# An S5 scan with a sparse feed-forward: one weight block by a turning transfer, selected tokens turned by a transfer

## The chip, the cores and the metric

The kernel runs on one core of a Trainium2 chip. The core has five engines with queues of their own: PE (TensorE, matrix products; the profile gives its weight loads apart as PEld), DVE (VectorE), ACT (ScalarE), POOL (GpSimd) and SP (SyncE), which here only issues transfers. Transfers ("DMA") run on 16 DMA engines. The metric is device time in microseconds (us). Three runs of the kernel before took 252.46, 252.49 and 252.91 us; the median is 252.49 us.

## The reference

Input `A_x` has 2048 tokens of width 1024. All arrays are bfloat16.

```
xn  = layernorm(x)
# A: diagonal complex state space, P = 1024 states
Bu  = xn @ B_bar.T                       # complex, 2048 x 1024
h_t = Lam_bar * h_(t-1) + Bu_t           # scan over the tokens
yA  = 2 * Re(h @ C.T) + xn * Dskip
# B: feed-forward for the 2 tokens with the greatest xn @ w_r
idx = argsort(-(xn @ w_r))[:2]
y   = (silu(xn[idx] @ w_gate) * (xn[idx] @ w_up)) @ w_down * sigmoid(r[idx])
yB  = xn;  yB[idx] += y
out = x + yA + yB
```

## The kernel before, in words

The 2048 tokens are cut into 16 chunks `c` of 128 tokens, and two chunks make one of 8 frames `f`. The names below are the task names of the table `ORDER`; a task is one small function that emits a few instructions, and the program is emitted in the order of that table. Each engine works its own instructions off in that order, so one late input holds up all that stands behind it on the engine.

For each chunk `x.c` loads the tokens, `bs.c`, `bn.c` and `rstd.c` (chunks 0 to 5; for the others `sum.c` and `sq.c` on ACT) find mean and variance, and `apply.c` writes the normalized tokens `xn`. They are turned, so that features lie on partitions: chunks 0 to 3 by products with the identity on PE (`Tpe.c`, emptied by `xnT.c` on ACT), the others by a turning transfer from SP (`T.c`).

The weights `B` are needed turned as well: `BT[ri][j]`, with `ri` 0 for the real and 1 for the imaginary part, and `j` for one of 8 blocks of 128 states. Tasks `B.j.ri` with `j` from 1 load them with a turning transfer (`load_B`, L235, the operation DMA_TRANSPOSE). Block 0 comes by two plain transfers into `Bn` (L176); `tB.ri` turns each part with 8 products on PE (L257) and `B.0.ri` copies it out of PSUM on ACT (L260). The weights `C` are loaded by four larger turning transfers (`C.dh.ri`, L240).

`Bu.f.j` (L668) is the product for one frame and one block of states: 16 matmuls. `u.f.j` copies it out of PSUM, `TI.f` rotates it (L723, L725), `SC.c.ri` is the scan along the tokens (L751; L744 in the last chunk), `gb.c.ri` narrows it, `TO.c` rotates back (L793, L795) and `Y.c.q` (L880) is the product with `C`: four quarters of 8 matmuls a chunk. The carry from chunk to chunk goes through POOL (`cw`, `cy`, `cin`). The output is seeded in PSUM by ACT (`seed`), and `xm.c` (L870) and `ADD.c.dh` (L891) on DVE, and `out.c.dh` (L895) finish it.

For part B, `r.0` and `r.1` are the router's products, and `cand` and `idx` on DVE find the two tokens (L941 to L979). `gather` fetches their rows, `bns` (L284, L286), `rstds` and `norm` (L1014) normalize them, `sT` turns them with 8 small products on PE (L1020) into PSUM, and `xT` on DVE clears the tile `xselT` and copies the turned rows in (L1026, L1027). `mm.i` are the products with the three large weights (L1068 gate and up, L1099 down); their tiles `w.n` are loaded from SP (L1056) into four slots that earlier tiles must have left. The result must reach the output rows of two tokens that are known only at run time. For all chunks but the last ones `fix` on POOL adds it in memory, by an indirect transfer (L1118) that waits for the stores of these chunks. For the last ones (`c >= UPD_C`) a one-hot matrix `hot` (L983 to L987) adds it in PSUM, by a product `hotY.c.dh` (L885); their stores wait for `fix`. `UPD_C` is 14, so chunks 14 and 15 go this way.

Of the kernel before, what the change touches and what calls it, by code (L numbers as in the profile page):

```python
# [29 lines left out]
xnT.3 bs.5 Bh.1.0.0 B.5.0 first Bh.1.0.1 u.0.2 Bu.1.0 cos B.4.1 Bu.1.1 bn.5 bs.4 sin bn.4 B.5.1 u.1.0 Bu.1.2 log B.6.0 den nmean.5 nmean.4 sq1.0 kappa  # L30
x.6 Bu.0.3 sq1.1 inv.0 u.1.1 rc.0 rstd.5 Bu.0.4 R0.0 rstd.4 apply.5 u.1.2 nmr.4 apply.4 T.5 inv.1 nmr.5 tan.0 Bu.1.3 nmr1.4 R.0 nmr.0 u.0.3 B.6.1 rc.1
u.0.4 ntan.0 Bu.1.4 tan.1 u.1.3 T.4 cs ntan.1 Bu.1.5 TI.0.0 xnT.5 Drow u.1.4 sum.7 B.7.0 Bu.1.6 nmean.7 u.1.5 B.7.1 ts.1.0 sq.7 cin.0.0 xnT.4 ends
ts.0.0 Bu.0.5 xr.0 ts.1.1 u.1.6 xr.1 sum.6 E2c.0 C.1.0 Bu.0.6 ts.0.1 nmean.6 sq.6 R0.1 R.1 rstd.6 Bu.0.7 SC.0.0.0 u.0.5 u.0.6 SC.0.0.1 cw.0.0 Bu.1.7
u.0.7 xs.0 E2s.1 C.0.0 cy.0.0 Bu.2.0 TI.0.4 seed.0.0 cin.1.0 u.1.7 seed.0.1 Bu.2.1 E2n.0 E2c.1 nmr.6 cin.0.4 u.2.0 nmr1.5 Bu.2.2 E2s.0 gb.0.0.1 C.0.1
u.2.1 SC.0.4.0 E2n.1 Bu.2.3 gb.0.0.0 SC.0.4.1 u.2.2 cw.0.4 rstd.7 gb.0.4.0 SC.1.0.0 Bu.2.4 cy.0.4 gb.0.4.1 SC.1.0.1 gb.1.0.0 cin.1.4 nmr.7 Bu.2.5
u.2.3 TO.0.0 u.2.4 apply.6 cw.1.0 Bu.2.6 apply.7 cy.1.0 TO.0.4 T.6 seed.1.0 Bu.2.7 x.8 u.2.5 SC.1.4.0 T.7 nmr1.7 Y.0.0 SC.1.4.1 gb.1.4.0 C.1.1 E2t.1
xm.0 E2t.0 cin.2.0 Y.0.1 TI.1.0 gb.1.0.1 xnT.6 xs.1 cw.1.4 Y.0.2 gb.1.4.1 cy.1.4 u.2.6 xnT.7 sum.8 Bu.3.0 x.9 cin.2.4 nmean.8 x.12 u.2.7 xr.3 sq.8
ADD.0.0 x.10 r.0 TO.1.0 out.0.0 rstd.8 Bu.3.1 seed.1.1 SC.2.0.0 u.3.0 xr.2 Bu.3.2 u.3.1 sum.9 SC.2.0.1 cw.2.0 Y.0.3 nmr1.8 gb.2.0.0 Bu.3.3 TO.1.4
gb.2.0.1 cy.2.0 nmr.8 apply.8 Bu.3.4 cin.3.0 xm.1 u.3.2 ADD.0.1 nmean.9 TO.2.0 sq.9 out.0.1 Y.1.0 T.8 rstd.9 u.3.3 x.11 Y.1.1 seed.2.0 xs.2 SC.3.0.0
Y.1.2 xnT.8 sum.12 Y.1.3 ADD.1.0 cw.3.0 u.3.4 SC.3.0.1 gb.3.0.0 out.1.0 Y.2.0 nmr.9 seed.2.1 xm.2 gb.3.0.1 cy.3.0 Y.2.1 ADD.1.1 nmean.12 TI.2.0  # L40
apply.9 out.1.1 cin.4.0 Bu.3.5 seed.3.0 T.9 sq.12 Bu.3.6 rstd.12 nmr.12 apply.12 Bu.3.7 SC.4.0.0 u.3.5 T.12 xnT.9 u.3.6 xs.3 Y.2.2 w.0 SC.4.0.1 cw.4.0
x.15 u.3.7 gb.4.0.0 Y.2.3 TO.3.0 gb.4.0.1 cy.4.0 xnT.12 Bu.4.0 sum.10 cin.5.0 nmean.10 sq.10 Bu.4.1 ADD.2.0 ADD.2.1 seed.3.1 Bu.4.2 SC.5.0.0 out.2.1
rstd.10 out.2.0 nmr.10 nmr1.6 xr.4 u.4.0 Y.3.0 w.1 u.4.1 xr.5 u.4.2 xm.3 cw.5.0 sum.11 SC.5.0.1 Y.3.1 nmean.11 sq.11 Y.3.2 ADD.3.0 cy.5.0 apply.10
TO.4.0 out.3.0 gb.5.0.0 Bu.4.3 T.10 cin.6.0 gb.5.0.1 Y.3.3 u.4.3 rstd.11 TI.3.0 seed.4.0 Bu.4.4 xnT.10 seed.4.1 nmr1.9 sum.15 Bu.4.5 nmr.11 nmean.15
xs.4 Bu.4.6 ADD.3.1 SC.6.0.0 out.3.1 seed.5.0 xr.6 u.4.4 Y.4.0 u.4.5 apply.11 SC.6.0.1 cw.6.0 Y.4.1 gb.6.0.0 T.11 sq.15 x.13 TO.5.0 Y.4.2 cy.6.0 x.14
gb.6.0.1 rstd.15 cin.7.0 Y.4.3 nmr.15 apply.15 xnT.11 xm.4 Bu.4.7 ADD.4.0 ADD.4.1 seed.5.1 SC.7.0.0 Y.5.0 xs.5 u.4.6 xr.7 Bu.5.0 sum.13 T.15 SC.7.0.1
cw.7.0 w.2 Y.5.1 u.5.0 w.3 u.4.7 w.4 xm.5 cy.7.0 seed.6.0 out.4.1 TO.6.0 Y.5.2 w.5 nmean.13 sq.13 cin.8.0 xnT.15 gb.7.0.1 Y.5.3 rstd.13 nmr.13 ADD.5.0
nmr1.13 Bu.5.1 gb.7.0.0 TI.4.0 sum.14 Bu.5.2 u.5.1 nmean.14 apply.13 Y.6.0 sq.14 T.13 SC.8.0.0 Bu.5.3 rstd.14 u.5.2 nmr1.11 nmr.14 Y.6.1 SC.8.0.1
cw.8.0 u.5.3 apply.14 xnT.13 Bu.5.4 gb.8.0.0 T.14 ADD.5.1 cy.8.0 TO.7.0 out.5.1 Bu.5.5 u.5.4 out.4.0 cin.9.0 out.5.0 Bu.5.6 u.5.5 gb.8.0.1 xnT.14
Bu.5.7 TO.8.0 u.5.6 Bu.6.0 u.5.7 xs.6 r.1 nmr1.10 xm.6 u.6.0 seed.6.1 ADD.6.0 Bu.6.1 cand xs.7 xr.8 w.6 seed.7.0 w.7 Y.6.2 out.6.0 u.6.1 nmr1.12  # L50
seed.7.1 Y.6.3 idx Y.7.0 xm.7 gather sig ADD.6.1 sig1 out.6.1 seed.8.0 Bu.6.2 SC.9.0.0 xr.9 Y.7.1 SC.9.0.1 gb.9.0.0 Y.7.2 xs.8 cw.9.0 ADD.7.0 gb.9.0.1
Bu.6.3 TI.5.0 cy.9.0 out.7.0 seed.8.1 u.6.2 Y.7.3 cin.10.0 u.6.3 Bu.6.4 bns Y.8.0 u.6.4 ADD.7.1 rstds xm.8 out.7.1 Bu.6.5 norm xr.10 SC.10.0.0 Y.8.1
xs.9 cw.10.0 sT nmr1.14 Bu.6.6 u.6.5 xT SC.10.0.1 seed.9.0 mm.0 TO.9.0 gb.10.0.1 cy.10.0 Y.8.2 w.8 gb.10.0.0 w.9 ymb0 w.10 u.6.6 w.11 Y.8.3 cin.11.0
w.12 xm.9 ADD.8.0 Bu.6.7 ADD.8.1 seed.9.1 SC.11.0.0 out.8.1 seed.10.0 Y.9.0 w.13 out.8.0 SC.11.0.1 Y.9.1 gb.11.0.0 cw.11.0 mm.1 ADD.9.0 gb.11.0.1
cy.11.0 TO.10.0 Y.9.2 seed.10.1 w.14 cin.12.0 exp.0 w.15 w.16 w.17 Bu.7.0 u.6.7 w.18 xs.10 w.19 gu.0 xr.11 Bu.7.1 u.7.0 out.9.0 gT.0 hot TI.6.0 Bu.7.2
u.7.1 Y.9.3 u.7.2 mm.2 ADD.9.1 SC.12.0.0 Bu.7.3 w.20 exp.1 out.9.1 xr.12 seed.11.0 w.21 Y.10.0 SC.12.0.1 cw.12.0 w.22 w.23 w.24 Y.10.1 w.25 xm.10
gb.12.0.1 cy.12.0 TO.11.0 Y.10.2 u.7.3 gb.12.0.0 cin.13.0 xs.11 Y.10.3 ADD.10.0 Bu.7.4 ADD.10.1 gu.1 xm.11 mm.3 u.7.4 SC.13.0.0 Bu.7.5 w.26 w.27
out.10.0 SC.13.0.1 gb.13.0.0 cw.13.0 out.10.1 Bu.7.6 w.28 seed.11.1 w.29 seed.12.0 w.30 gT.1 Bu.7.7 cy.13.0 xr.13 exp.2 TO.12.0 w.31 u.7.5 cin.14.0
Y.11.0 gb.13.0.1 u.7.6 xs.12 Y.11.1 gu.2 gT.2 mm.4 ADD.11.0 TO.13.0 seed.12.1 Y.11.2 w.32 exp.3 w.33 out.11.0 u.7.7 xr.14 Y.11.3 nmr1.15 w.34 w.35
Y.12.0 ADD.11.1 xm.12 out.11.1 seed.13.0 TI.7.0 Y.12.1 mm.5 Y.13.0 w.36 w.37 ADD.12.0 w.38 SC.14.0.0 w.39 Y.12.2 w.40 w.41 out.12.0 Y.12.3 SC.14.0.1  # L60
gb.14.0.0 cw.14.0 seed.13.1 Y.13.1 gu.3 gb.14.0.1 cy.14.0 gT.3 ADD.12.1 Y.13.2 xs.13 TO.14.0 cin.15.0 seed.14.0 Y.13.3 mm.6 xm.13 ADD.13.0 mm.7
# [1119 lines left out]
```

## Time and profile before

| | |
|---|---|
| median of three runs | 252.49 us |
| the profiled execution, whole | 252.6 us |
| its span, first to last instruction | 250.8 us |
| PE busy | 244.7 us, 98% |
| DVE busy | 238.7 us, 95% |
| ACT busy | 176.0 us, 70% |
| POOL busy | 103.1 us, 41% |
| granted TensorE clock | 1.000 of full speed (the level of 2.4 GHz) |

Times in the rows are counted from the span's start. The profiled execution lies 1.8 us above its span, and 0.1 us above the median of the runs. A share of busy time is a mean over the whole program; where an engine waits and for whom is read from the views below.

### The profile page before, as it was taken

Reading aid. Unit: us, or ns where it says so; the run is one execution under the profiler, and the core shown is the slowest. Engines: PE = TensorE matmul, PEld = TensorE weight load, DVE = VectorE, ACT = ScalarE, POOL = GpSimd, SP = SyncE. Lnnn points to the kernel's source line nnn. Section 1 sums busy time; section 2 is a strip of 40 time slices with the busy share of each in tenths; the row PEclk is TensorE's granted clock in tenths of the full one; section 3 lists DMA queues with packets and bytes.
Section 4 is the critical chain, followed back from the end, with each engine's and each line's share of the span. In section 5 each row is a group of like instructions: output and inputs, shape, how many; then the busy total and the mean of one; then the engine's idle time right before and its main releaser. Section 6 shows DMA issues by size and latency. Waiting matters only on the chain.

```text
span 250.8 us, 5086 instructions
## 1 busy us (share of the span) xinstructions
PE 244.7 (98%) x1995; PEld 165.3 (66%) x1995; DVE 238.7 (95%) x284; ACT 176.0 (70%) x303; POOL 103.1 (41%) x132
## 2 busy tenths in 40 slices
...
GB/s 206 248 227 178 189 212 247 222 186 288 52 105 46 103 123 214 44 108 83 246 235 85 22 230 67 21 63 240 344 358 319 343 241 390 338 351 288 107 44 42
DMA packets 66532, 46.75 MB, mean 186 GB/s; under 512 B 45890, under 2 KB 52424, under 8 KB 66508
## 3 DMA queue, kind: packets, MB, share of 16 engines
...
q0 software_dynamic: 96, 0.01, 0.0%
...
## 4 chain that ended last, share of the span: by engine, by line
PE 84%; ACT 5%; DVE 5%; DMA 3%; SPq 1%; issue 0%
PE pY L880 44%; PE pB L668 35%; PE pG L1068 3%; DMA BT<-in_A_B_im_dram 2%; DVE st L310 1%; PE pD L1099 1%; ACT u L674 1%; DMA xt<-in_A_x_dram 1%; PE r_ps L409 1%; ACT xnT L395 1%; DVE ot L891 1%; DVE xn L339 1%; DVE E1t L551 1%; ACT L522 1%; ACT L519 1%; SPq L235 0%
## 5 line engine op out<-in xcount | busy, mean ns | idle before, releaser
L668 PE MATMUL pB<-xnT,BT 128*128 128x256 bf16 (+1 forms) x1072 | 116.3, 268 | 0.4 <-DMA BT<-in_A_B_im_dram 0.4
L880 PE MATMUL pY<-CT,hT 128*128 128x512 bf16 (+1 forms) x528 | 115.0, 373 | 0.0
L668 PEld LDWEIGHTS <-BT 128*128 128x128 bf16 x1072 | 100.4, 98 | 16.7 <-issue 1.3
L880 PEld LDWEIGHTS <-hT 128*128 128x128 bf16 x528 | 51.2, 98 | 55.0 <-issue 1.5
L767 POOL TENSOR_TENSOR cw<-gf,tL 128x16 f32<-128x16 f32 (+1 forms) x34 | 37.2, 1098 | 92.2 <-DVE gf L751 91.4
L751 DVE TENSOR_TENSOR_SCAN gf<-R,v 128x1040 f32<-128x1040 f32 (+1 forms) x34 | 68.6, 2055 | 0.3
L757 ACT CAST gb<-gf 128x1024 bf16<-128x1024 f32 (+1 forms) x34 | 31.7, 941 | 21.5 <-DVE gf L751 21.2
L674 ACT CAST u<-pB 128x512 bf16<-128x512 f32 x64 | 36.0, 579 | 12.8 <-PE pB L668 12.7
L856 ACT ACTIVATE pY<-xr,nmr_all,rstd_all 128x512 f32<-128x512 bf16 (+1 forms) x33 | 25.0, 763 | 14.7 <-DVE ot L891 11.4
L793 DVE TENSOR_TENSOR m<-gb,E 128x4096 bf16<-128x4096 bf16 x13 | 29.6, 2279 | 0.1
L891 DVE TENSOR_TENSOR ot<-pY,ot 128x512 bf16<-128x512 f32 (+1 forms) x33 | 21.4, 663 | 2.2 <-PE pY L880 1.3
L865 ACT ACTIVATE ot<-xr,nmr_all,rstd_all 128x1024 bf16<-128x1024 bf16 x16 | 19.8, 1238 | 1.9 <-DMA out_dram<-ot 1.8
L782 POOL CAST v<-cy 128x16 bf16<-128x16 f32 (+1 forms) x17 | 18.6, 1096 | 5.0 <-DVE gf L751 4.1
L795 DVE TENSOR_TENSOR hT<-m 128x2048 bf16<-128x2048 bf16 x13 | 15.9, 1225 | 0.4
L725 DVE TENSOR_TENSOR v<-u,m 128x4096 bf16<-128x4096 bf16 x7 | 16.0, 2292 | 0.2
L723 DVE TENSOR_TENSOR m<-u,E1t 128x4096 bf16<-128x4096 bf16 x7 | 16.0, 2283 | 0.0
L783 POOL TENSOR_TENSOR v<-cy,v 128x16 bf16<-128x16 f32 (+1 forms) x17 | 14.5, 851 | 1.4
L775 POOL TENSOR_TENSOR cy<-cw 128x16 f32<-128x16 f32 (+1 forms) x17 | 13.9, 816 | 1.3
L350 ACT ACTIVATE xn<-xt,nmr_all,rstd_all 128x1024 bf16<-128x1024 bf16 x10 | 12.3, 1237 | 0.1
L325 ACT ACTIVATE xn<-xt,nmean_all 128x1024 bf16<-128x1024 bf16 x10 | 11.5, 1146 | 0.2
L870 DVE TENSOR_TENSOR ot<-ot,Drow 128x1024 bf16<-128x1024 bf16 x16 | 10.9, 682 | 0.0
L319 ACT ACTIVATE xn<-xt 128x1024 bf16<-128x1024 bf16 x10 | 10.6, 1056 | 0.0
...
## 6 DMA issues: line engine op xcount, KB each, us to landing
...
out_dram<-ot SPq DMA_DIRECT2D x31, 128.0 KB, 1.7
...
xt<-in_A_x_dram SPq DMA_DIRECT2D x2, 128.0 KB, 2.3
...
```

The costliest lines, as they stand in the source:

```text
L668: nc.tensor.matmul(out=pB[:, ri, ts_], lhsT=BT[ri][j][:, k, :], rhs=xnT_frame(f)[:, k, ts_], start=(k == 0), stop=(k == DT - 1))
L674: nc.scalar.copy(out=u_tiles[f][:, :, :, j, :].rearrange("p c i t -> p i c t"), in_=pB_tiles.pop((f, j))[:].rearrange("p i (c t) -> p i c ...
L723: nc.vector.tensor_tensor(out=m[:].rearrange("p c i j t -> p c (i j t)"), in0=u[:].rearrange("p c i j t -> p c (i j t)"), in1=E1t[:].rearr ...
L751: nc.vector.tensor_tensor_scan(out=flat(gf), data0=flat(R[:, js, :]), data1=flat(v[:, ri, js, :]), initial=0.0, op0=ALU.mult, op1=ALU.add)
L757: nc.scalar.copy(out=gb_tiles[c][:, ri, js, :], in_=gf_tiles[c, js.start, ri][:, :, 2:])
L767: nc.gpsimd.tensor_tensor(out=cw_tiles[c, js.start][:, ri, :, 0:n], in0=g.unsqueeze(1).to_broadcast([128, 2, n]), in1=tL[:, ri, :, js], op ...
L782: nc.gpsimd.tensor_copy(out=v[:, :, js, 0], in_=cy[:, :, 0:n])
L793: nc.vector.tensor_tensor(out=m[:].rearrange("p k i j t -> p k (i j t)"), in1=E2[:].rearrange("p k i j t -> p k (i j t)"), in0=flat(gb[:]) ...
L856: nc.scalar.activation(out=pY[:, 0:d_.stop - d_.start], in_=y_tiles["xr", c][:, d_], func=ACT.Identity, bias=nmr_all[:, c:c + 1], scale=rs ...
L865: nc.scalar.activation(out=y_tiles["ot", c][:], in_=y_tiles["xr", c][:], func=ACT.Identity, bias=nmr_all[:, c:c + 1], scale=rstd_all[:, c: ...
L880: nc.tensor.matmul(out=pY, lhsT=h_tiles[c][:, ri, j, :], rhs=CT[ri][h][:, j, d0:d0 + w], start=False, stop=end, skip_group_check=True)
L891: nc.vector.tensor_add(out=ot, in0=y_tiles.pop(("pY", c, dh))[:, 0:d_.stop - d_.start], in1=ot)
```

## The change

Five things are changed together.

1. Only the real part of the first block of `B` comes by a plain transfer. The imaginary part `BT[1][0]` is loaded by a turning transfer from SP, as the other blocks are; `tB.1` and its copy on ACT go.
2. The selected tokens are turned by a transfer from SP (`sT`, out of 32 rows that `xz` on POOL clears beforehand); the 8 products on PE and the clearing and copying on DVE go.
3. `UPD_C` is 15: chunk 14 has no product with the one-hot matrix, `fix` waits for chunk 14's stores also, and only chunk 15's stores wait for `fix`.
4. The turned tile of chunk 1 lies in the PSUM slot `T`, no longer in one of the three slots of `Bu`. The statistics of chunks 2 to 5 stand behind `apply.1`.
5. The whole table `ORDER` is another one.

```diff
-xa x.0 Bn.0 Bn.1 start.0 warm.0 warm.1 warm.2 warm.3 warm.4 warm.5 warm.6 warm.7 bs.0 pre x.2 warm.8 B.1.0 x.1 bn.0 warm.9 warm.10 bs.1 rstd.0 nmean.0
+warm.0 warm.1 warm.2 warm.3 warm.4 warm.5 warm.6 warm.7 x.0 warm.8 warm.9 warm.10 warm.11 start.0 warm.12 xa bs.0 bn.0 x.1 warm.13 bs.1 rstd.0 applyA
...
-    Bn = work.tile([128, 2, D], BF16, name="Bn", tag=f"F{NSF}")
-    for ri in range(2):
-        nc.sync.dma_start(out=Bn[:, ri, :], in_=(A_B_re, A_B_im)[ri][0:128, :])
+    Bn = work.tile([128, D], BF16, name="Bn", tag=f"F{NSF}")
+    nc.sync.dma_start(out=Bn[:], in_=A_B_re[0:128, :])
...
-    for ri in range(2):
-        add(("Bn", ri), "none", 5.45 + 0.65 * ri, lambda: None, key=-1, takes=[(f"F{NSF}", "Bn", [("tB", 0), ("tB", 1)])])
...
+    add(("Bn", 0), "none", 5.45, lambda: None, key=-1, takes=[(f"F{NSF}", "Bn", [("tB", 0)])])
+    add(("tB", 0), "PE", 0.45, turn_B, [("Bn", 0), ("warm", NWARM - 1), ("pP", 0)], key=-60, takes=[("pB", ("tB", 0), [("B", 0, 0)])])
+    add(("B", 0, 0), "ACT", 1.0, evac_B, [("tB", 0)], key=-60)
+    add(("B", 0, 1), "SP", 1.35, lambda: load_B(1, 0), [("pre",)], key=-89.92, mb=0.31, lag=1.2)
...
-        pT_tiles[c] = psum.tile([128, DT, 128], BF16, name="pT", tag="B" if c == 1 else "misc" if odd else "T", bufs=3 if c == 1 else 1)
+        pT_tiles[c] = psum.tile([128, DT, 128], BF16, name="pT", tag="misc" if odd and c > 1 else "T")
...
-    UPD_C = NCH - CPF
+    UPD_C = NCH - 1
...
+    def sel_zero():
+        ms["xnsel"] = xnp.tile([128, D], BF16, name="xnsel", tag="xn")
+        nc.gpsimd.memset(ms["xnsel"][0:32, :], 0.0)
+
     def sel_T():
-        ms["pX"] = psum.tile([128, DT, 2], BF16, name="pX", tag="misc")
-        for j in range(DT):
-            nc.tensor.transpose(out=ms["pX"][:, j, :], in_=ms["xnsel"][:, j * 128:(j + 1) * 128], identity=ident[0:2, 0:2])
-
-    def sel_xT():
         mw = xin.tile([128, D], BF16, name="mw", tag="xt")
...
-        nc.vector.memset(ms["xselT"], 0.0)
-        nc.vector.tensor_copy(out=ms["xselT"][:, :, 0:2], in_=ms["pX"][:])
+        nc.sync.dma_start_transpose(out=ms["xselT"], in_=ms["xnsel"][0:32, :].rearrange("t (do di) -> t do di", di=128))
```

**What the new order moves on SP at the start.** Transfers as SP issues them, from the second token chunk on; `BT_j` is block `j` (the number behind it is the tile's), `xt` a chunk of tokens. Before:

```order
L165 DMA xt<-in_A_x_dram 128x1024
L176 DMA Bn<-in_A_B_re_dram 128x1024
L176 DMA Bn<-in_A_B_im_dram 128x1024
L231 DMA xt<-in_A_x_dram 128x1024
L235 DMA_TRANSPOSE BT_1_116<-in_A_B_re_dram 128x8x128
L231 DMA xt<-in_A_x_dram 128x1024
L235 DMA_TRANSPOSE BT_1_124<-in_A_B_im_dram 128x8x128
L235 DMA_TRANSPOSE BT_2_117<-in_A_B_re_dram 128x8x128
L235 DMA_TRANSPOSE BT_2_125<-in_A_B_im_dram 128x8x128
L231 DMA xt<-in_A_x_dram 128x1024
```

And now, from the same transfer on:

```order
L164 DMA xt<-in_A_x_dram 128x1024
L174 DMA Bn<-in_A_B_re_dram 128x1024
L229 DMA xt<-in_A_x_dram 128x1024
L233 DMA_TRANSPOSE BT_0_122<-in_A_B_im_dram 128x8x128
L233 DMA_TRANSPOSE BT_1_115<-in_A_B_re_dram 128x8x128
L229 DMA xt<-in_A_x_dram 128x1024
L233 DMA_TRANSPOSE BT_1_123<-in_A_B_im_dram 128x8x128
L233 DMA_TRANSPOSE BT_2_116<-in_A_B_re_dram 128x8x128
L233 DMA_TRANSPOSE BT_2_124<-in_A_B_im_dram 128x8x128
L233 DMA_TRANSPOSE BT_5_119<-in_A_B_re_dram 128x8x128
L229 DMA xt<-in_A_x_dram 128x1024
```

One plain transfer has gone, and one turning transfer has come in ahead of the other blocks; the next chunk of tokens (`x.5` before, `x.4` now) stands one block later.

**On SP up to the last block of B.** From `B.5.1` to `B.7.1`; `xnT<-xn` are `T.5` and `T.4`, `Drow` is the row `Dskip`. Before:

```order
L235 DMA_TRANSPOSE BT_5_128<-in_A_B_im_dram 128x8x128
L235 DMA_TRANSPOSE BT_6_121<-in_A_B_re_dram 128x8x128
L231 DMA xt<-in_A_x_dram 128x1024
L401 DMA_TRANSPOSE xnT<-xn 128x8x128
L235 DMA_TRANSPOSE BT_6_129<-in_A_B_im_dram 128x8x128
L401 DMA_TRANSPOSE xnT<-xn 128x8x128
L861 DMA Drow<-in_A_Dskip_dram 128x1024
L235 DMA_TRANSPOSE BT_7_122<-in_A_B_re_dram 128x8x128
L235 DMA_TRANSPOSE BT_7_130<-in_A_B_im_dram 128x8x128
```

And now:

```order
L233 DMA_TRANSPOSE BT_5_127<-in_A_B_im_dram 128x8x128
L399 DMA_TRANSPOSE xnT<-xn 128x8x128
L233 DMA_TRANSPOSE BT_6_120<-in_A_B_re_dram 128x8x128
L233 DMA_TRANSPOSE BT_6_128<-in_A_B_im_dram 128x8x128
L399 DMA_TRANSPOSE xnT<-xn 128x8x128
L233 DMA_TRANSPOSE BT_7_121<-in_A_B_re_dram 128x8x128
L233 DMA_TRANSPOSE BT_7_129<-in_A_B_im_dram 128x8x128
```

`Drow` stands behind the last block now, and chunk 6's tokens (`x.6`) ahead of this piece.

**On DVE around TO.8 and the choice of tokens.** L793 with L795 is a `TO` (L791 with L793 in the changed kernel), L941 begins `cand`, the scans are called gf<-R,v. Before, from `TO.7`:

```order
L793 TENSOR_TENSOR m<-gb,E_136 128x4096
L795 TENSOR_TENSOR hT<-m 128x2048
L793 TENSOR_TENSOR m<-gb,E_136 128x4096
L795 TENSOR_TENSOR hT<-m 128x2048
L870 TENSOR_TENSOR ot<-ot,Drow 128x1024
L891 TENSOR_TENSOR ot<-pY,ot 128x512
L941 COPY rs<-r_ps 8x256
```

And now, from the end of `idx` (L977), which before comes behind this `TO.8`:

```order
L977 CAST idx_t<-tok 32x1
L868 TENSOR_TENSOR ot<-ot,Drow 128x1024 x2
L889 TENSOR_TENSOR ot<-pY,ot 128x512 x2
L749 SCALAR_TENSOR_TENSOR gf<-R,v 128x1040 x2
L791 TENSOR_TENSOR m<-gb,E_135 128x4096
L793 TENSOR_TENSOR hT<-m 128x2048
L282 BN_STATS st<-xsel 2x6 x2
L284 BN_AGGR mv<-st 2x2
L889 TENSOR_TENSOR ot<-pY,ot 128x512 x2
L868 TENSOR_TENSOR ot<-ot,Drow 128x1024
L1011 TENSOR_SCALAR xnsel<-xsel,mv,rstd_s 2x1024
```

`TO.8` has moved behind the whole choice of the tokens and behind both scans of chunk 9, and `norm` follows it closely.

## Rows read from the trace of the kernel before

**Rows 1.** Busy time in one stretch: length, then each engine's busy us.

```profile
25.00:215.00 190.00, 189.64 (x1476) 128.58 (x1474) 187.30 (x196) 144.08 (x250) 88.13 (x92) 1.00 0.65 182
```

**Rows 2.** Timeline of PE, start: start us, us, instructions, idle before and who ended it.

```profile
8.24 0.62 PE L383 MATMUL pT<-ident,xn 128*128 128x128 bf16 x8 [0.62 <-DVE xn L339]
...
12.90 1.15 PE L383 MATMUL pT<-ident,xn 128*128 128x128 bf16 x16 [0.38 <-DVE xn L339]
```

**Rows 3.** Waits of PE: us in total, times, longest.

```profile
PE pB L668 <- DMA BT<-in_A_B_im_dram: 0.4, 1, 0.4
```

**Rows 4.** The chain of work that ended last, in order of time: start us, us.

```profile
30.58 5.66 DMA BT<-in_A_B_im_dram
...
36.28 16.77 PE pB L668 x152
...
166.34 0.28 PE pX L1020 x8
166.62 1.85 PE pB L668 x16
...
200.77 1.41 PE pG L1068 x24
...
239.72 0.65 PE pY L885 x3
```

**Rows 5.** Timeline of SP: start us, us that the issue took.

```profile
2.61 0.43 SPq L176 DMA_DIRECT2D Bn<-in_A_B_im_dram  x1
...
23.06 0.52 SPq L231 DMA_DIRECT2D xt<-in_A_x_dram  x1
...
23.81 2.10 SPq L401 DMA_TRANSPOSE xnT<-xn  x1
...
28.67 0.57 SPq L861 DMA_DIRECT2D Drow<-in_A_Dskip_dram  x1
...
30.58 2.15 SPq L235 DMA_TRANSPOSE BT<-in_A_B_im_dram  x1
```

**Rows 6.** Tile BT: issue duration ns min/median/max, and landing counted from the issue.

```profile
L235 SPq DMA_TRANSPOSE BT<-in_A_B_re_dram x7: 1237/1308/2298, 3.6 to 29.3; - x7
...
DMA to landing us min/median/max: 3.3/4.6/5.7
```

**Rows 7.** Timeline of DVE: start us, us.

```profile
141.91 1.23 DVE L795 TENSOR_TENSOR hT<-m 128x2048 bf16<-128x2048 bf16 x1
...
144.45 0.40 DVE L941 COPY rs<-r_ps 8x256 f32<-8x256 f32 x1
...
152.21 4.54 DVE L751 TENSOR_TENSOR_SCAN gf<-R,v 128x1040 f32<-128x1040 f32 x2
...
161.78 1.27 DVE L284 BATCH_NORM_STATS2 st<-xsel 2x6 f32<-2x512 bf16 x2
...
164.36 0.53 DVE L1014 TENSOR_SCALAR xnsel<-xsel,mv,rstd_s 2x1024 bf16<-2x1024 bf16 x1
...
239.97 1.29 DVE L891 TENSOR_TENSOR ot<-pY,ot 128x512 bf16<-128x512 f32 x2 [0.55 <-PE pY L885]
```

**Rows 8.** Timeline of PE around the selected tokens.

```profile
160.98 1.89 PE L880 MATMUL pY<-CT,hT 128*128 128x512 bf16 x8
...
168.41 1.48 PE L1068 MATMUL pG<-wt,mw 128*32 128x512 bf16 x24
```

**Rows 9.** Two weight tiles at 201.4 us: issues, and the second's landing from its issue.

```profile
L1056 SPq DMA_DIRECT2D wt<-in_B_w_up_dram x1: 1344/1344/1344, 201.8 to 201.8; - x1
...
DMA to landing us min/median/max: 6.6/6.6/6.6
```

**Rows 10.** Issues of transfers: number, KB each, median us to landing.

```profile
out_dram<-ot SPq DMA_DIRECT2D x31, 128.0 KB, 1.7
...
out_dram<-ymb,idx_t POOLq DMA_INDIRECT x1, 2.8
```

More of the change, by code (lines that the diff above doesn't have):

```diff
@@ L30 @@
[L30 to L61, printed above, removed]
@@ new lines @@
+apply.0 bn.1 warm.14 warm.15 TpeA xnT.0 Bn.0 rstd.1 pP.0 pcol.0 wr dt tB.0 B.0.0 Tpe.0 xnT0 apply.1 frq nmean.1 nmean.0 nmr1.0 nmr.1 rad pre x.2 B.0.1
+B.1.0 Tpe.1 xnT.1 Bh.0.0.0 Bh.0.0.1 bs.2 bn.2 Bh.0.1.0 Bu.0.0 nmean.2 rstd.2 x.3 bs.3 bn.3 nmean.3 rstd.3 trig nmr.3 B.1.1 Bh.0.1.1 Bu.0.1 apply.2
+Tpe.2 nmr1.2 apply.3 Tpe.3 B.2.0 B.2.1 nmr1.3 u.0.0 u.0.1 turns Bu.0.2 xnT.2 Bh.1.0.0 Bh.1.0.1 B.5.0 whole angle x.4 bs.4 xnT.3 Bu.1.0 Bu.1.1 B.3.0
+abs B.3.1 sin nmr.0 nmr.2 u.0.2 Bu.1.2 first u.1.0 cos log x.5 den bn.4 kappa sq1.1 sq1.0 x.6 Bu.0.3 bs.5 rstd.4 apply.4 x.7 nmr1.1 bn.5 u.1.1 inv.0
@@ new lines @@
+u.2.2 cin.0.4 gb.0.0.0 cy.1.0 gb.0.0.1 T.6 xnT.6 E2n.0 E2s.0 SC.0.4.0 xnT.7 x.8 seed.0.0 SC.0.4.1 u.2.3 Bu.2.5 Bu.2.6 E2n.1 TO.0.0 cw.0.4 cy.0.4
+gb.1.0.0 u.2.4 cin.1.4 gb.1.0.1 u.2.5 gb.0.4.1 Drow Bu.2.7 Bu.3.0 TO.1.0 gb.0.4.0 SC.1.4.0 cw.1.4 SC.1.4.1 cin.2.0 TO.0.4 u.2.6 sum.8 seed.0.1 u.2.7
+nmean.8 sum.9 Bu.3.1 Bu.3.2 Y.0.0 gb.1.4.0 Y.0.1 r.0 E2t.1 TI.1.0 C.1.0 Y.0.2 gb.1.4.1 C.1.1 Y.0.3 nmean.9 xs.0 seed.1.0 sq.9 u.3.0 u.3.1 Bu.3.3 u.3.2
+E2t.0 cy.1.4 cin.2.4 SC.2.0.0 gb.2.0.0 rstd.9 nmr1.9 nmr.9 apply.9 SC.2.0.1 gb.2.0.1 TO.1.4 sq.8 xs.1 x.10 nmr1.5 xm.0 ADD.0.0 seed.1.1 T.9 xr.2
```

73 lines of the change are left out of this document (47 added, 26 removed).

## The prediction, made before the changed kernel ran

> **What bounds the kernel now.** I read the stretches first. From 25 to 215 us PE is busy for 189.64 of 190 us and DVE for 187.30 [rows 1]. Both are full, so neither shares nor means help; what matters is who ever makes PE wait. The list of PE's waits has one wait for a transfer, 0.4 us for a block of B [rows 3], and the timeline of the start has two for normalized tokens, 0.62 us before 8.24 and 0.38 before 12.90 [rows 2]. The chain of waits puts these together: it runs through SP's transfers to the landing of the last block of B (issued 30.58, landed 36.24), and from 36.28 it is PE work almost without a break to the last products [rows 4]. So the time is: landing of B.7.1, plus the PE work behind it, plus a tail. DVE is nearly as full, and where it comes late it will add to that sum. I therefore ask three things: when does B.7.1 land, how much PE work goes from behind it, and who comes late in the new order.
>
> **The start.** The second turning of block 0 on PE (`tB.1`) goes, but it lies ahead of the 0.62 us in which PE waits for tokens anyway [rows 2]. Worth nothing; its cover is the normalization of chunk 1, which the change leaves as it is. In the new order the two-step statistics of chunks 2 and 3 go straight to their `apply`, with the angle table behind them, so the 0.38 us before 12.90 should go. What is late next is the block of B: PE would reach it 0.38 earlier and wait longer.
>
> SP issues these transfers one by one, so I compare what it issues up to B.7.1. Added: one turning transfer, 1.24 to 1.31 us in most cases [rows 6] and about 0.05 to the next, 1.35. Removed: the plain transfer of the imaginary part, 0.48 with its gap, and `Drow`, which now stands behind, 0.62 [rows 5]. SP's own wait ahead of the transfer at 23.81 is 0.23 (the issue before it ended at 23.58) and goes, since `T.4` now comes later than its input; I put 0.2 for other small gaps (an estimate). 1.35 - 0.48 - 0.62 - 0.23 - 0.2 = -0.2 us. Bounds: some of the turning issues take 2.1 to 2.3 us without a wait that the profile names [rows 5, 6]; one more such would be +0.9. On the other side PE cannot start earlier than it is ready: 0.4 + 0.38 = -0.8 [rows 2, 3]. I take -0.2.
>
> The row says that a turned block holds SP for three times as long as a plain one (1.24 against 0.43) [rows 5, 6]. The Trainium skill, "Advanced Engine Details and Errata", section "X-Bar Transpose (TRN2)", says that transposing transfers are as fast as regular ones. Here the trace disagrees for the issue. By the rule the added transfer would cost 0.48 like the removed one, B.7.1 would come 0.9 earlier than I have it, and this term would be at its bound of -0.8; it is a rival below.
>
> The added transfer also delays `x.4` and with it chunk 4's statistics, which stand on DVE ahead of the table's `abs`. It costs nothing as long as ACT's cosine, behind a table load, is what DVE waits for next; without that cover DVE is some tenths later at chunk 0, where PE now has three products (`Bu.3.0` to `Bu.3.2`) more to do first.
>
> **The selected tokens.** The 8 small products take 0.28 us on the chain, and the `Bu` behind them takes 1.85 instead of 16.77 / 9.5 = 1.77 [rows 4]: -0.36 us of PE work. On DVE the clearing and the copy go; PE does not wait for DVE there, so I book nothing.
>
> In their place SP issues one transfer, whose price the trace does not show (32 rows instead of 128). It must land before `mm.0`. PE: `mm.0` began at 168.41 [rows 8]; two `Bu` and the small products stand behind it now, 168.41 - 3.5 - 0.36 = 164.5. DVE: see the rival on DVE for 155.6 as the end of `TO.8`; behind it come `bns` (1.5 with its second step), three instructions of 0.6 and `norm` (0.53) [rows 7], so `norm` ends at 159.4. Turned blocks land 3.3 to 5.7 us after their issue [rows 6]: 162.7 to 165.1. Below that the price is nothing, above it PE waits up to 0.6 us. I take 0, because a quarter of the bytes is nearest to the lower end. Behind this waiting transfer SP holds `xr.9` and the next weights; `xr.9` is for chunk 9, whose products come 5 us after `mm.0`, and the weight slots open only with `mm.0`.
>
> **Chunk 14 without the one-hot product.** Three products take 0.65 us on the chain, one after the other [rows 4]; two go: -0.43 us. DVE's 0.55 us of waiting for them [rows 7] goes too, which keeps DVE's lead over PE in the last chunk although PE comes earlier. The price would be `fix`, which now waits for chunk 14's stores. Chunk 14's second add ended at 239.97 + 1.29 = 241.3; without the wait it ends some 1.2 earlier, its store lands 1.7 later and `fix` 2.8 after that [rows 7, 10], together about 244.6. Only the last chunk's stores wait for it, and their adds come after the last products, which began with 239.72 + 0.65 and run some 7 us. Two us of cover; price 0.
>
> **What the order adds on PE.** `mm.6` and `mm.7` are parted by two products of Y; a change from one kind to another costs about 0.08 (1.85 against 1.77). And `mm.4` comes soon after `mm.3`: 1.41 + two quarters of Y + one `Bu`, 6.6 us, where four more tasks lay between before. Its second weight tiles are asked for when `mm.3` has left their slot: in the trace 0.6 us after `mm.3` began (200.77), and they landed 6.6 us after the second issue at 201.78, so 7.6 us after `mm.3` began [rows 4, 9]. `mm.4` needs them half a us after its own start, at 7.1. So PE waits 0.5 if the queue is as full as then, 0 if it is emptier; it should be, as the loads before them start earlier. I take +0.2, range 0 to 0.7.
>
> **Sum.** -0.2 - 0.36 - 0.43 + 0.08 + 0.2 = -0.7 us. The profiled execution took 252.6 us (span 250.8 and 1.8 around it): 251.9. It lies 0.1 above the median of the runs, 252.49, against which a time will be read: 251.8 us.
>
> **Rivals.**
>
> *B.7.1 is early enough.* If the turning transfer costs SP what a plain one does (the rule above), or one of the long issues falls away, PE no longer waits at the block: -0.8 instead of -0.2, so 251.2 us. For it: the long issues are no property of the transfer, their number may change. Against it: none of the 14 turned blocks took less than 1.24 [rows 6].
>
> *No change.* One more long issue puts B.7.1 0.9 later than I have it, +0.7 in place of -0.2; the 0.7 saved behind it is used up: 252.6 us, 252.7 with the wait at `mm.4`, 252.4 without. For it: SP issues 17 turned transfers instead of 16 up to there, and about one in four took over 2 us.
>
> *Slower: DVE is late at chunk 8.* `TO.8` ended at 143.1 and `Y.8.0` began at 160.98 [rows 7, 8], a lead of 17.8 us. Now `cand`, `idx`, the finishing work of chunk 6 and both scans of chunk 9 stand ahead of `TO.8`: from 144.45 to 152.21 + 4.54, less `sig1` and with two more short instructions, 12.5 us [rows 7]. It ends at 155.6, while PE, with two `Bu` fewer ahead, is there at 160.98 - 3.5 = 157.5. The lead is 1.9 us, and DVE has no slack to make a loss good [rows 1]; on the way stand a wait for `r.1` (PE) and the early ones for `x.4` and the cosine. Every us lost beyond 1.9 is PE's, and over 3.1 the kernel is slower than before by 0.5. At 3.5: 251.8 + 1.6 = 253.4 us. Against it: the sum of the waits that I can place is under 1 us.
>
> **How the numbers follow.** My forecast 0.50, its own range 251.2 to 252.4; early block 0.14; no change 0.20; DVE late 0.16. A measurement of this kernel tells 0.2% (0.5 us) from no change, that is 252.0 to 253.0. Of the forecast's half 0.40 lies below 252.0 and 0.10 above it. Faster: 0.40 + 0.14 = 0.54. Same: 0.10 + 0.19 = 0.29. Slower: 0.16 and 0.01 of the third case, 0.17. The range runs from 250.9 (the early block with no wait at `mm.4` and a little more) to 253.3, just short of the late DVE's price; it leaves out under 0.2.
>
> **What would show it.** In the chain of waits of the changed kernel: a BT transfer before PE's long run, landing between 35.5 and 37.1; no pX row; one L883 row of one product instead of three; PE's end about 0.9 us earlier against that landing. In the list of PE's waits: xn at the start gone from the second place, BT at about 0.6 us; a wait of a weight product for wt of under 0.7. A PE wait for mw would show the turned tokens late, a wait of pY<-CT,hT for DVE around 157 or 169 us would show the slower rival. It would be wrong altogether if PE's waits after 40 us summed to over 1 us, or if the clock's rows were not at their full level throughout as before.

## The result, and the profile after

The changed kernel took 254.81 us (median of 8 runs, 254.55 to 255.17), the kernel before, beside it, 252.97. The ratio is 1.0084 (95% interval 1.0063 to 1.0106): 0.84% slower. Forecast were 251.8 us with a range of 250.9 to 253.3, so the time lies outside the range and on the other side. The profiled execution took 254.64 us with a span of 252.9, 2.1 longer than the span before. The granted clock of that execution is 1.000, its full level.

PE has less work than before (243.9 us busy instead of 244.7) and ends later. The page says who holds it up. Its busy lines of PE and DVE, and the shares of the chain of work that ended last:

```profile
PE 243.9 (96%) x1977; PEld 163.7 (65%) x1977; DVE 239.7 (95%) x281; ACT 175.1 (69%) x302; POOL 95.7 (38%) x133
...
DVE 60%; PE 12%; POOL 8%; DMA 7%; issue 6%; SPq 3%; ACT 2%; DVEq 0%; POOLq 0%
```

The same line of the page before:

```profile
PE 84%; ACT 5%; DVE 5%; DMA 3%; SPq 1%; issue 0%
```

Then the chain was PE's. Now it runs through DVE. PE's waits (us in total, times, longest) answer to [rows 3]; the first of the list, 1.4 us at the very start, is the same in both kernels and left out:

```profile
PE pY L878 <- DVE hT L793: 1.3, 1, 1.3
PE pT L381 <- DVE xn L337: 1.0, 1, 1.0
PE pY L878 <- ACT pY L854: 0.6, 2, 0.3
PE pY L878 <- DVE hT L800: 0.5, 1, 0.5
PE pB L666 <- DMA BT<-in_A_B_im_dram: 0.4, 1, 0.4
PE pT L386 <- DVE xn L344: 0.4, 1, 0.4
```

Where they lie is in the timeline of PE (start, us, instructions, idle before and who ended it), to be read beside [rows 2, 8]:

```profile
8.09 0.62 PE L381 MATMUL pT<-ident,xn 128*128 128x128 bf16 x8 [1.02 <-DVE xn L337]
...
13.80 26.43 PE L666 MATMUL pB<-xnT,BT 128*128 128x256 bf16 x256
...
146.95 1.89 PE L878 MATMUL pY<-CT,hT 128*128 128x512 bf16 x8 [0.30 <-ACT pY L854]
...
152.16 5.34 PE L878 MATMUL pY<-CT,hT 128*128 128x512 bf16 x24
158.79 3.63 PE L878 MATMUL pY<-CT,hT 128*128 128x512 bf16 x16 [1.28 <-DVE hT L793]
...
165.84 1.48 PE L1064 MATMUL pG<-wt,mw 128*32 128x512 bf16 x24
...
243.13 1.03 PE L878 MATMUL pY<-CT,hT 128*128 128x256 bf16 x8 [0.26 <-ACT pY L854]
244.00 0.38 PE L883 MATMUL pY<-ymb,hot 128*128 128x512 bf16 x1
...
247.45 1.04 PE L878 MATMUL pY<-CT,hT 128*128 128x512 bf16 x4 [0.46 <-DVE hT L800]
```

Three things are to be seen. From 13.80 us on PE has no wait for a block of B in 26.43 us, where the forecast had 0.6; ahead of that it waits 0.4 for one. The row of 158.79 is the slower rival's place: `Y.8.0` waits for `TO.8`. And there are waits at the very end, for the last rotation on DVE. Such a row understates a break: a product of 512 columns is shown with 0.38 us (x496, mean 379 ns), but the next starts 0.216 behind it (24 in 5.34 us), so 0.16 is to be added. So the four breaks behind 40 us are 0.46, 1.44, 0.42 and 0.62; a fifth, 0.28 from start to start, lies at `Y.9.0` and is too short for a row of its own. Together 3.2 us. The prediction had named both signs: a wait of `Y` for DVE around 157 us would show the slower rival, and over 1 us of waits behind 40 us would make it wrong altogether.

DVE around `TO.8`, as in [rows 7]:

```profile
117.83 0.71 DVE L868 TENSOR_TENSOR ot<-ot,Drow 128x1024 bf16<-128x1024 bf16 x1
118.65 1.29 DVE L889 TENSOR_TENSOR ot<-pY,ot 128x512 bf16<-128x512 f32 x2
...
150.76 4.53 DVE L749 TENSOR_TENSOR_SCAN gf<-R,v 128x1040 f32<-128x1040 f32 x2
155.21 2.27 DVE L791 TENSOR_TENSOR m<-gb,E 128x4096 bf16<-128x4096 bf16 x1
157.51 1.23 DVE L793 TENSOR_TENSOR hT<-m 128x2048 bf16<-128x2048 bf16 x1
...
235.72 2.95 DVE L742 TENSOR_TENSOR_SCAN gb<-R,v 128x520 bf16<-128x520 f32 x3
```

Two pairs and the first scan of chunk 15 in the kernel before; in the first pair the `xm` is followed by the add of another chunk, in the second by a scan:

```profile
68.02 0.69 DVE L870 TENSOR_TENSOR ot<-ot,Drow 128x1024 bf16<-128x1024 bf16 x1
68.63 0.68 DVE L891 TENSOR_TENSOR ot<-pY,ot 128x512 bf16<-128x512 f32 x1
...
94.99 0.67 DVE L870 TENSOR_TENSOR ot<-ot,Drow 128x1024 bf16<-128x1024 bf16 x1
95.57 2.35 DVE L751 TENSOR_TENSOR_SCAN gf<-R,v 128x1040 f32<-128x1040 f32 x1
...
233.22 3.54 DVE L744 TENSOR_TENSOR_SCAN gb<-R,v 128x520 bf16<-128x520 f32 x4
```

`TO.8` ends at 158.7; the forecast had 155.6. So DVE had lost 3.1 us on the way. To find them I took, for each task on DVE, the time from its start to the next task's start, in both traces, and added up the same tasks, all that stand ahead of `TO.8` and itself: 152.8 us before, 155.8 now, 3.0 more. By the start of chunk 15's scans the sum is 3.2. What has gone from DVE (clearing and copying the turned tokens, one one-hot instruction) is 0.5, the first task counted starts 0.2 earlier, and so the first scan of chunk 15 starts 2.5 us later (235.72; 233.22 before). Between 50 and 235 us DVE is never idle for more than 0.2 us at a stretch, so nothing there could take the lag back. The 3.0 are in two halves:

- Up to 49 us, 1.5: a wait of 0.84 for chunk 4 and some ten pieces of 0.1 to 0.3, less two waits of before, 1.0 for the cosine and 0.4 for a product. Of these only the wait for chunk 4 was put to a test below.
- From there to `TO.8`, 1.5: an instruction that is followed directly by the one that reads its result. `xm` takes 0.58 to 0.61 from start to start where something else follows, 0.79 to 0.82 where the add of the same chunk follows (118.65 - 117.83 above). That the follower is an add is not the reason: behind `xm.1` in the kernel before it is one too, of chunk 0, and 0.61 passes. `TI` takes 4.53 and 4.74. Net of such places in the kernel before, five `xm` and two `TI` got such a neighbour by the new order: 7 x 0.21.

### The profile page after: what moved, and what is told of

It is laid out like the page before. It is cut to its first block, busy times and chain, and to the rows that moved or that the text cites. A ratio compares the mean times of both kernels' runs of the same rounds, so it can differ in the third digit from the quotient of the medians.

```text
span 252.9 us, 5065 instructions
## 1 busy us (share of the span) xinstructions
PE 243.9 (96%) x1977; PEld 163.7 (65%) x1977; DVE 239.7 (95%) x281; ACT 175.1 (69%) x302; POOL 95.7 (38%) x133
## 4 chain that ended last, share of the span: by engine, by line
DVE 60%; PE 12%; POOL 8%; DMA 7%; issue 6%; SPq 3%; ACT 2%; DVEq 0%; POOLq 0%
DVE gf L749 18%; DVE m L791 6%; DVE ot L889 6%; PE pB L666 6%; PE pY L878 5%; DMA out_dram<-ot 4%; DVE v L723 4%; DVE m L721 4%; DVE ot L868 3%; POOL cw L765 3%; DMA xt<-in_A_x_dram 2%; POOL v L780 2%; POOL v L781 2%; DVE hT L793 2%; DVE gb L742 2%
## 5 line engine op out<-in xcount | busy, mean ns | idle before, releaser
L765 POOL TENSOR_TENSOR cw<-gf,tL 128x16 f32<-128x16 f32 (+1 forms) x34 | 41.9, 1231 | 108.0 <-DVE gf L749 107.3
L791 DVE TENSOR_TENSOR m<-gb,E 128x4096 bf16<-128x4096 bf16 x13 | 29.5, 2272 | 0.0
L793 DVE TENSOR_TENSOR hT<-m 128x2048 bf16<-128x2048 bf16 x13 | 15.9, 1225 | 0.4
L780 POOL CAST v<-cy 128x16 bf16<-128x16 f32 (+1 forms) x17 | 12.4, 728 | 1.2
L781 POOL TENSOR_TENSOR v<-cy,v 128x16 bf16<-128x16 f32 (+1 forms) x17 | 12.3, 721 | 1.4
L773 POOL TENSOR_TENSOR cy<-cw 128x16 f32<-128x16 f32 (+1 forms) x17 | 11.6, 680 | 1.3
```

What stands on the lines that cost most here:

```text
L765: nc.gpsimd.tensor_tensor(out=cw_tiles[c, js.start][:, ri, :, 0:n], in0=g.unsqueeze(1).to_broadcast([128, 2, n]), in1=tL[:, ri, :, js], op ...
L791: nc.vector.tensor_tensor(out=m[:].rearrange("p k i j t -> p k (i j t)"), in1=E2[:].rearrange("p k i j t -> p k (i j t)"), in0=flat(gb[:]) ...
L793: nc.vector.tensor_add(out=hT[:].rearrange("p i j t -> p i (j t)"), in0=m[:, 0].rearrange("p i j t -> p i (j t)"), in1=m[:, 1, ::-1].rearr ...
```

## The experiments

Two theories were set against each other. D: the sum of DVE's durations and waits sets the end; the place of `TO.8` only is where it shows first. P: only that place costs, and the rest of the time is PE's work. Medians in us, with the kernel before on the same chip beside each:

| run | median | before | ratio, 95% interval |
|---|---|---|---|
| e1_parted | 252.32 | 252.87 | 0.9974 (0.9952 to 0.9996) |
| e2_x4_early | 254.43 | 252.87 | 1.0064 (1.0040 to 1.0087) |
| e3_TO8_early | 258.52 | 252.87 | 1.0230 (1.0189 to 1.0270) |
| e4_old_order_two_parts | 251.82 | 252.87 | 0.9949 (0.9930 to 0.9968) |
| e5_TO8_ahead_of_scans | 258.31 | 252.82 | 1.0222 (1.0185 to 1.0259) |
| e6_parted_more | 251.85 | 252.82 | 0.9957 (0.9928 to 0.9985) |
| e7_old_order_three_parts | 252.65 | 252.82 | 0.9991 (0.9970 to 1.0013) |
| e8_TO8_and_seed_early | 254.74 | 252.78 | 1.0075 (1.0059 to 1.0092) |
| e9_parted_more_plain_block | 251.63 | 252.78 | 0.9954 (0.9936 to 0.9973) |
| changed_again | 254.76 | 252.78 | 1.0066 (1.0042 to 1.0090) |
| e10_before_joined | 253.83 | 252.74 | 1.0040 (1.0016 to 1.0064) |

In the diffs below stands the order of the tasks on the engine that is named; the other engines keep theirs. Where several engines are changed, a diff is cut and names them in brackets.

**Neighbours parted.** Three of the ten places, on DVE:

```diff
-TO.4.0 xm.3 ADD.3.0 TI.3.0 SC.6.0.0 SC.6.0.1 ADD.3.1 TO.5.0 xm.4 ADD.4.0
+xm.3 TO.4.0 ADD.3.0 TI.3.0 ADD.3.1 SC.6.0.0 SC.6.0.1 xm.4 TO.5.0 ADD.4.0
```

> The changed kernel with ten DVE neighbours parted: xm (or the second step of TI) no longer stands directly ahead of the instruction that reads its result; nothing else moves. Theory D (DVE's own sum sets the end: a direct reader costs 0.2 us): 8 of the 10 pairs lie ahead of TO.8, so TO.8 ends 1.6 us earlier (157.2 instead of 158.8), PE's wait of 1.28 for it is gone, and the end comes 1.9 us earlier: 252.9 us. Theory P (only the place of TO.8 costs, PE's work sets the end else): the same wait goes, 1.3 us: 253.5. If a direct reader costs nothing: 254.8, as the changed kernel.

2.4 us less than the changed kernel, by the same work on every engine: a lower time than either theory had, and nearer to D (252.9) than to P (253.5). In its trace the pair shown above reads so, `xm` with `TO.5` behind it, and `TO.8` ends at 157.3; PE has no wait there any more:

```profile
113.25 0.67 DVE L868 TENSOR_TENSOR ot<-ot,Drow 128x1024 bf16<-128x1024 bf16 x1
113.83 2.31 DVE L791 TENSOR_TENSOR m<-gb,E 128x4096 bf16<-128x4096 bf16 x1
...
156.09 1.22 DVE L793 TENSOR_TENSOR hT<-m 128x2048 bf16<-128x2048 bf16 x1
```

0.58 instead of 0.82 from start to start. Task by task, the ten places gave 0.18 to 0.24 each, and 0.11 came back at `xm.7`, which now stands ahead of an add in place of `xm.6`. The sum over all of DVE is 2.2 less, and so is the span (250.7; 252.9).

**The same in the other kernel, the other way round.** The kernel before, with ten `xm` moved to stand directly ahead of their add:

```diff
-ADD.2.1 SC.5.0.0 xm.3 SC.5.0.1 ADD.3.0 TO.4.0
+ADD.2.1 SC.5.0.0 SC.5.0.1 xm.3 ADD.3.0 TO.4.0
```

> The kernel before with nothing changed but ten places on DVE: xm.0 to xm.3, 5, 7 and 9 to 12 moved to stand directly ahead of the add that reads their result. Theory D (a direct reader costs 0.2 us, and DVE's sum counts): DVE is 2.0 us later at the end; 0.55 of that is its wait for the one-hot product of chunk 14, 0.4 the lead of TO.15.6 (244.99) over its product (245.41), the rest is PE's: 1.0 us slower, 253.9 against 252.8. If a direct reader costs nothing: no change.

1.1 us slower, as worked out. The pair, from start to start 0.77 instead of the 0.58 to 0.61:

```profile
98.13 0.67 DVE L870 TENSOR_TENSOR ot<-ot,Drow 128x1024 bf16<-128x1024 bf16 x1
98.90 0.69 DVE L891 TENSOR_TENSOR ot<-pY,ot 128x512 bf16<-128x512 f32 x1
```

So the price of a direct reader is shown in both kernels, and that DVE, which hardly showed in the chain before, had only about one us to give.

**The x.4 wait.** On SP:

```diff
-B.2.0 B.2.1 B.5.0 x.4 B.3.0
+B.2.0 B.2.1 x.4 B.5.0 B.3.0
```

> The changed kernel with one move on SP: x.4 ahead of B.5.0 instead of behind it, 1.9 us earlier. Theory D: DVE's wait of 0.84 for x.4 goes and everything on DVE comes 0.8 earlier down to the end: 254.0 us, TO.8 at 158.0, PE's wait for it 0.5. Rival: the cosine on ACT, behind its table load, is waited for next and takes most of it back: 254.6.

By the medians 0.3 to 0.4 us less (against 254.76 and 254.81); the intervals overlap, so the time alone shows neither theory wrong. The trace does: the first scan of chunk 15 starts 0.36 earlier (235.36), not 0.8, which is the rival. DVE's wait for `x.4` is gone, but the cosine is what it waits for next:

```profile
15.35 0.68 DVE L308 BATCH_NORM_STATS2 st<-xt 128x6 f32<-128x512 bf16 x1
...
19.20 1.29 DVE L536 TENSOR_TENSOR th<-cf 128x512 f32<-128x512 f32 x2 [0.93 <-ACT cf L532]
```

In the changed kernel:

```profile
16.39 0.69 DVE L308 BATCH_NORM_STATS2 st<-xt 128x6 f32<-128x512 bf16 x1 [0.84 <-DMA xt<-in_A_x_dram]
...
19.57 1.29 DVE L536 TENSOR_TENSOR th<-cf 128x512 f32<-128x512 f32 x2 [0.25 <-ACT cf L532]
```

The first comes 1.04 earlier, the second 0.37: the cosine takes 0.67 back.

**The place of TO.8.** Three tries, since the first two broke something else. On DVE:

```diff
-xm.5 ADD.5.0 ADD.5.1 cand idx ... SC.9.0.0 SC.9.0.1 TO.8.0
+xm.5 ADD.5.0 ADD.5.1 TO.8.0 cand idx ... SC.9.0.0 SC.9.0.1
```

> The changed kernel with one move on DVE: TO.8 behind ADD.5.1, ahead of the choice of the tokens, about 12 us earlier. PE's wait of 1.28 before Y.8.0 goes under both theories. Theory P (the place alone): the end comes 1.3 earlier, 253.5 us. Theory D (DVE's sum sets the end): PE is ahead of DVE then and waits later, at the half chunks of chunk 15; the sum of DVE is what it was: 254.5 to 254.8 us, with PE's waits of 1.3 found again behind 165 us.

Neither: 3.7 us slower. ACT's `sig` waits for the choice of the tokens, which is now later, and the seeds of PSUM stand behind it on ACT:

```profile
ACT sig L995 <- DVE sel L970: 5.1, 1, 5.1
...
PE pY L878 <- ACT pY L854: 5.7, 2, 3.3
```

Part of the 3.7 goes with the granted clock: it was 0.987 to 0.993 in five of the six runs, and the sixth, at 1.000, took 258.04. The experiment tells nothing on D and P. Next, `TO.8` behind the choice, but ahead of the two scans:

```diff
-ADD.6.0 ADD.6.1 SC.9.0.0 SC.9.0.1 TO.8.0 bns
+ADD.6.0 ADD.6.1 TO.8.0 SC.9.0.0 SC.9.0.1 bns
```

> The changed kernel with one move on DVE: TO.8 ahead of the two scans of chunk 9 instead of behind them, so it ends 4.5 us earlier, at 154.3; nothing else of the order is touched and ACT's queue only gets the scans' copies later. PE's wait of 1.28 before Y.8.0 goes under both theories. Theory P (the place alone): the end comes 1.3 earlier than the changed kernel, 253.5 us. Theory D (DVE's sum sets the end): PE waits as much later, for TO.9 and at the half chunks of chunk 15: 254.6 us, DVE's last steps where they were.

Again slower, with times from 256.31 to 260.26, of which the lowest is the profiled one. There `Y.8.0` waits for its seed, which stands on ACT behind the copies of the two scans (the expectation had left that out), and there is a wait for a block of C that the edit does not explain:

```profile
66.14 1.89 PE L878 MATMUL pY<-CT,hT 128*128 128x512 bf16 x8 [2.00 <-DMA CT<-in_A_C_im_dram]
161.52 3.61 PE L878 MATMUL pY<-CT,hT 128*128 128x512 bf16 x16 [2.13 <-ACT pY L854]
```

Inconclusive. The spread goes with the granted clock: 256.31 at 0.998, 257.86 and 257.93 at 0.993, and 258.70 to 260.26 at 0.987 and 0.984; why the clock was lower there is open, as only the first was traced. The third has the same move on DVE and one on ACT:

```diff
-u.6.2 xs.8 gb.9.0.1 gb.9.0.0 seed.8.0 rstds
+u.6.2 seed.8.0 xs.8 gb.9.0.1 gb.9.0.0 rstds
```

> The changed kernel with TO.8 ahead of the two scans of chunk 9, as in the run before, and seed.8.0 ahead of xs.8 and the scans' copies on ACT, so that neither DVE nor ACT is late for Y.8.0. PE's wait of 1.28 before Y.8.0 goes. Theory P (the place alone): the end comes 1.3 earlier than the changed kernel, 253.5 us. Theory D (DVE's sum sets the end): TO.9 ends at 171.0 as in the changed kernel, PE waits 1.3 for it there instead, and the end stays: 254.6 us.

254.74 against 254.76 of the changed kernel on the same chip, as D has it. PE's waits behind 40 us in the profiled execution, and the first scan of chunk 15:

```profile
66.11 1.89 PE L878 MATMUL pY<-CT,hT 128*128 128x512 bf16 x8 [2.03 <-DMA CT<-in_A_C_im_dram]
247.42 1.04 PE L878 MATMUL pY<-CT,hT 128*128 128x512 bf16 x4 [0.45 <-DVE hT L800]
...
235.70 1.82 DVE L742 TENSOR_TENSOR_SCAN gb<-R,v 128x520 bf16<-128x520 f32 x2
```

The time alone doesn't decide between the theories: the wait for `TO.8` is gone, but PE lost 2.0 us for C elsewhere, and its breaks behind 40 us add up to 3.1, nearly what they were (3.2). What speaks for D is DVE's own times. The first scan of chunk 15 starts at 235.70 (235.72 in the changed kernel), DVE is nowhere idle for more than 0.2 us between 50 and 235 us in either, and PE waits for the last rotation at 247.42 (247.45). Had PE not waited for C, it would have stood there earlier and waited longer; that last step is argued, not run.

> The changed kernel itself, beside the other two on the same chip: 254.8 us, PE's wait for TO.8 1.3 and no wait for a block of C (the kernel with TO.8 ahead of the scans had one of 2.0 at 66 us, far ahead of its edit).

254.76, with the wait for `TO.8` of 1.29 and none for C. The profiled execution is the slowest of the four, 255.54: from 8 to 12 us its granted clock was near the lower level (0.62, then 0.53 of full speed), and the first scan of chunk 15 started 0.9 later than in the other trace. The wait for C came in two of the four kernels whose first 140 us are the same; in both, SP's issue of the first block of C took long, 6.4 and 6.8 us (4.9 in e3_TO8_early, 5.7 and 4.2 in the two traces of the changed kernel). Why, is open; as one and the same kernel has 5.7 and 4.2, it isn't the order alone.

**The parts without the new order.** The kernel before with `sT` and `UPD_C` 15 alone:

```diff
-... norm ... sT (PE) xT (DVE) ... xm.14 fix hotY.14.0 hotY.14.1 ADD.14.0
+... xz (POOL) norm ... sT (SP) ... xm.14 ADD.14.0 ADD.14.1 out.14.0 out.14.1 fix
```

> The kernel before, its order kept, with two parts of the change alone: selected tokens turned by a transfer (sT) and UPD_C 15. By the terms of the prediction: -0.36 and -0.43 of PE work, DVE 0.5 us shorter: 252.0 us against 252.8 (0.8 less than the kernel before). Rival: the turned tokens land behind PE's arrival at mm.0 (168.1) and eat 0.3 to 1 of it, or fix is late: 252.5 to 253.5.

1.05 us less than before (0.8 to 1.8 by the interval). Then with the turned block as well:

```diff
-Bn.0 Bn.1 x.2 B.1.0 ... tB.0 tB.1
+Bn.0 x.2 B.0.1 B.1.0 ... tB.0
```

> The kernel before, its order kept, with all three parts: sT by a transfer, UPD_C 15, and the imaginary part of block 0 by a turning transfer directly ahead of B.1.0. By the term of the prediction (a turned block holds SP 1.35 where the plain one took 0.48): every later block and token chunk 0.87 later, B.7.1 too, PE waits that much more: 0.9 above the kernel with two parts, 252.7 us. If the start hides it: 251.8.

0.83 of it is lost again by the medians: SP's price of a turned block, 0.87, fits in the old order. Its trace has a wait of 1.3 on DVE for a chunk of tokens (at most 0.6 with the two parts) and one of 0.68 on PE for the copy of a product, and none of PE for the last block of B; so the price seems to be paid at the former:

```profile
23.84 29.85 PE L667 MATMUL pB<-xnT,BT 128*128 128x256 bf16 x272 [0.68 <-ACT u L673]
```

**Towards a better one.** Four more pairs parted and `x.4` early:

```diff
-R.1 R.0 SC.0.0.0 ... TI.7.0 SC.14.0.0 xm.12 ADD.12.0 ... xm.13 ADD.13.0 ADD.13.1 SC.15.0.0
+R.0 R.1 SC.0.0.0 ... TI.7.0 xm.12 SC.14.0.0 ADD.12.0 ... xm.13 SC.15.0.0 ADD.13.0 ADD.13.1
```

> The kernel with ten parted pairs, and on top: TI.7 and xm.12 parted from SC.14 and ADD.12.0, xm.13 from ADD.13.0, R.0 from the first scan (4 pairs, 0.8 us), and x.4 ahead of B.5.0 (0.3). Theory D: DVE ends up to 1.1 earlier, but PE had only 0.5 us of waits left behind 40 us; the end moves by 0.4 to 0.6: 251.8 us. If DVE doesn't bound there any more: 252.3, as with the ten.

251.85, as worked out, though its interval overlaps that of e1_parted. PE's waits are all at the start now, so the bound is PE again:

```profile
PE warm L412 <- POOL ident masks.py:199: 1.4, 1, 1.4
PE pT L381 <- DVE xn L337: 1.0, 1, 1.0
PE pB L666 <- DMA BT<-in_A_B_re_dram: 0.5, 1, 0.5
PE pB L666 <- DMA BT<-in_A_B_im_dram: 0.3, 1, 0.3
```

Last, this one with the plain transfer of the imaginary part and `tB.1` back:

```diff
-Bn.0 x.2 B.0.1 (SP) B.1.0 ... tB.0 Tpe.0 Tpe.1
+Bn.0 Bn.1 x.2 B.1.0 ... tB.0 Tpe.0 tB.1 B.0.1 (ACT) Tpe.1
```

> The kernel with fourteen parted pairs and the early x.4, with the first part of the change undone: the imaginary part of block 0 by a plain transfer and 8 products on PE (tB.1). By SP's price of a turned block (0.87) all blocks come 0.9 earlier, PE's waits for blocks (0.55 and 0.25) go and the products of tB.1 lie in PE's wait of 1.0 for tokens: 251.1 us. If the waits only move to the tokens or to the copy on ACT: 251.8.

251.63, only 0.2 less where 0.7 was expected, and the intervals of the two overlap: the waits for blocks shrink from 0.8 to 0.2, and one of 0.4 for the copy of the turned block on ACT comes in their place. It beats both kernels (0.46% below before, interval 0.27 to 0.64), as do e4_old_order_two_parts and e6_parted_more; the three can't be told apart.

## Why the prediction was wrong

**The step that failed** is the one that set DVE's lead at chunk 8. The place was right: PE, by the forecast, reaches `Y.8.0` at 157.5, and the row has it at 158.79 with a wait of 1.28 ahead, which is 157.51. That this fits so closely is partly luck: PE was 0.6 early at 40 us and lost 0.46 of it waiting for a seed at 146.95. But `TO.8` was put at 155.6 with a lead of 1.9 us, on the ground that "the sum of the waits that I can place is under 1 us", and so the sum of the forecast had nothing for DVE. It ended at 158.7, 3.1 later. The lead was mis-sized in two ways. Durations were taken from rows as if an instruction cost the same whatever follows it; seven new direct readers cost 1.5 us. The rows of before show the price to whoever reads starts and not durations. And the waits at the start came to 1.5 us more, not under 1.

**The price of the rival was too small** (253.4 for a loss of 3.5 us; for the loss of 3.1 it gives 253.0, and 254.8 was measured). It counted one break of PE, at `Y.8.0`. But a DVE that has no idle time stays late to the end, and the lead of the rotations in chunk 15 is only 0.4 us: it breaks PE there again, whatever has been won in between. The whole lag of DVE in chunk 15, less that lead, is the right price: 2.5 - 0.4 = 2.1, which is the measured difference of the spans. Its chance, 0.16, was too low for a move that took a lead from 17.8 to 1.9 us on an engine with 187.30 busy of 190.

**Term by term, where PE is concerned, the forecast was right or too careful.**

- *B.7.1*, -0.2 (bounds -0.8 to +0.9): it was issued at 30.70, with no wait of PE. By 40.2 PE has done 320 products of `Bu` (64 up to 12.9 and the 256 of the row above), before 314 by its timeline: at 0.11 each some 0.6 earlier. That is the rival of the early block, in the new order; in the old one the added transfer costs 0.83. The rule in the Trainium skill, "Advanced Engine Details and Errata", section "X-Bar Transpose (TRN2)", that turning transfers are as fast as plain ones, would have the same cost of nothing in both orders: e7_old_order_three_parts speaks against it, and no turned block here was issued in under 1.24 us.
- *Selected tokens*, -0.36, and *chunk 14*, -0.43: the two parts gave 1.05 together in the old order, 0.26 more than the sum, inside the interval. `sT` was issued at 162.38 and `mm.0` started at 165.84 without a wait, so the 0 for its landing holds here; in e7_old_order_three_parts PE waits 0.2 for it. `fix` was hidden, as forecast, but it landed at 248.6 and not at 244.6, only 0.6 ahead of the end of chunk 15's first add (249.2); the forecast had two us.
- *mm.4*, +0.2: no wait; 0.
- *The delay of x.4*: "costs nothing as long as ACT's cosine ... is what DVE waits for next". It cost 0.4 of DVE's time: the cosine covers 0.67 of 1.04.

**What a direct reader costs, and a rule for it.** An instruction that doesn't need the result starts 0.09 before the end of the `xm` ahead of it (113.25 + 0.67 against 113.83), the reader of the result 0.11 behind it (117.83 + 0.71 against 118.65). The Trainium skill, "VectorE: DVE Perf Modes", section "The DRAIN you can't avoid", says that the next instruction starts when the pipe is empty, and earlier if it is not held; the two rows agree with that. For a row of copies the same section reports that a semaphore after each cost nothing extra. Taken as a rule for readers it does not fit here: the ten parted pairs would have changed nothing, and they gave 2.4 us. What in the engine makes the reader later, no run here shows.
